# Block-causal attention and a feed-forward pair: the values product of 48 heads taken from whole fp32 operands, two heads side by side

## The chip, the core and the metric

The program runs on one core of one Trainium2 chip. The metric is the device time of one execution in microseconds (us), the median of three runs. One further execution was recorded by the hardware profiler; every row of the trace below is from that one. The engines are TensorE (PE, its weight loads PEld), VectorE (DVE), ScalarE (ACT), GpSimd (POOL) and SyncE (SP), which here only issues DMAs.

## The reference

Eight batches of eight heads, 576 positions, head size 64. Position i sees position j when i's block of 64 is not before j's. The result goes through two dense layers with a leaky ReLU between them:

```
scores = scale * q @ k.T                    # (8, 8, 576, 576), scale = 1/8
scores = where(block_i >= block_j, scores, -1e9)
attn   = exp(scores - max); attn /= sum + 1e-9
x      = attn @ v  -> (4608 tokens, 512)
out    = leaky(x @ w_in) @ w_out            # 512 -> 2048 -> 512, slope 0.01
```

All inputs are fp32.

## The kernel before

**Split operands.** TensorE takes fp32 data in two ways here. An fp32 matmul shows as two matmul records. An "fp32r" matmul shows as one record but keeps fewer bits, so an operand is first split into a high part (a copy into fp32r) and a low part (value minus high part), and a product is built of the partial products. The dense layers work with split operands throughout (`wih`, `wil`, `xh`, `xl`, `gh`, `gl`).

**Heads.** The first 16 heads (`PLAIN`) use whole fp32 operands in the score product (L492) and in the values product (L675); the latter takes two heads at once: head z multiplies with 64 stationary columns and writes PSUM partitions 64z to 64z+63 (`paired`). The other 48, called split heads here, form the scores from split q and k (L503). Their softmax is by DVE (maximum, L524), ACT (exponential, L533) and one of POOL, ACT or DVE (normalising, L562 to L564). The probabilities are turned in 32 x 32 blocks by DVE (L706, tile `turn`), go through DRAM in four DMAs out (L723, `way<-turn`) and four back (L730, `ptm<-way`), and lie in `ptm` with the key on the partitions. Then `ptm` (L738, L739) and the values `v_stage` (L483, L484) are split: four casts and four subtractions per head for `ptm` into `pt`, one of each for `v_stage` into `vs`. These operations have the lines of their helpers in the profile: L263 is a copy or cast on ACT, L264 one on DVE, L273 a subtraction on DVE, L274 one on POOL. The values product of one head is ten fp32r matmuls (L637, L639) with 128 stationary columns (64 of the high part of v, 64 of the low part), so PSUM holds two halves that have to be added: one reduction (L280), two copies (L263 or L264) and four additions (L623, L657) per head bring them into `xr`. There is one `turn`, one `ptm`, one `pt`, one `vs` and one `v_stage`, used by every split head in turn.

**Dense layers.** Tokens go through in 18 chunks of 256. A chunk can start when the batch that holds its last token has been through all eight heads. L793 is the first layer, 3456 matmuls of 256 columns; L820 the second, 1728 of 512.

**The order.** The program is written out by `Plan`, a list scheduler that runs when the kernel is built: each operation has a rank (lower goes first), alternatives by engine, and a modelled duration. Constants set ranks and margins: `RP` for the preparation of q and k, `RT` for the turning, `RM` for its DMAs, `RV` and `RX` for the values product and what follows it, `LEAD` and `LAG` for the dense layers, `PADD` for the margin that it adds after a DMA before it treats an operation as safe to place. Every engine works off its own list strictly in the written order: whatever waits at the head holds up all behind it. SP's list of DMAs is such a list too.

Of the kernel before, what the change touches and what calls it, by code (L numbers as in the profile page):

```python
# [36 lines left out]
RL = -2.043  # L37
RP = 13.059
RB = -31.003
RT = 3.126  # L40
RV = 0.737
RX = 1.288
RN = -97.836
RM = -7.716
RC = 5.009

LEAD = 5.093
LAG = 1.993
RS = -19.813
RG = 1.33  # L50
OFF1 = 3.023
SL1 = 26.175
AHEAD = 2.181
# [5 lines left out]
PADD = 1454.095  # L59
HOLD = 92.996  # L60
FILL = 235
FILLTO = -161.364
# [3 lines left out]
PAD = 426.427  # L66
PADO = 56.068
SPARE = 36.345
CHANGE = 100
RATE = 0.449  # L70
SLOW = 8000


class Plan:
# [37 lines left out]
    def run(self):  # L112
# [14 lines left out]
        start, stream, halved = 0, 0, False  # L127
# [40 lines left out]
        while done < total:  # L168
# [6 lines left out]
            for e, q in ready.items():  # L175
# [29 lines left out]
                name, cost, fn = choices[k]  # L205
# [41 lines left out]
def attention_ffn(ctx: ExitStack, tc: tile.TileContext, q2: bass.AP, k2: bass.AP, qk: bass.AP, v: bass.AP, w_in: bass.AP, w_out: bass.AP, out: bass.AP):  # L247
# [114 lines left out]
    def second_stage():  # L362
        coded.close()
        pool = ctx.enter_context(tc.tile_pool(name="late", bufs=1, side="right", reuse_waits="tile"))
        later["qs"] = fixed([P, S], F32R, "qs", 2, pool)
        later["ks"] = fixed([P, 2, S], F32R, "ks", None, pool)
        later["vs"] = fixed([P, NT, 2 * D], F32R, "vs", None, pool)
        later["v_stage"] = fixed([P, NT, D], F32, "v_stage", None, pool)

    def third_stage():  # L370
        early.close()
        pool = ctx.enter_context(tc.tile_pool(name="last", bufs=1, reuse_waits="tile"))
        later["pt"] = fixed([P, 2, turned], F32R, "pt", None, pool)
        later["ptm"] = fixed([P, turned], F32, "ptm", None, pool)
        later["turn"] = fixed([P, turned], F32, "turn", None, pool)
        xh.append(fixed([P, ND, CH], F32R, "xh1", None, pool))

    def weight_piece(num, rank, f, out_side, c0):
# [28 lines left out]
        if src.dtype != F32:  # L407
# [4 lines left out]
            add([("SP", 475, load)], rank - AHEAD, [], [r_key, t_key], lag="raw")  # L412
# [17 lines left out]
        else:  # L430
# [4 lines left out]
            add([("SP", 475, load)], rank - AHEAD, [], [v_key], lag="raw")  # L435
# [3 lines left out]
    def attention(i):  # L439
# [17 lines left out]
        if plain:  # L457
            kt = lambda: k_in[:, d % 2]
            if z == 0:
                add([("SP", 475, lambda: nc.sync.dma_start(kt(), k2[d]))], early_load, [], [("k", d % 2)], lag="k")  # L460
                add(copying(S, kt, kt, by=scale), rp, [], [("k", d % 2)])
            half = slice(64 * z, 64 * z + 64)
            add([("SP", 475, lambda: nc.sync.dma_start(qk_in[half, z], q2[d, half]))], early_load + 0.05, [], [("q", z)], lag="q")
            vt, vkey = lambda: vf[z], ("vf", z)
            qkd = [("k", d % 2), ("q", z)]
        else:
            add([("SP", 475, lambda: nc.sync.dma_start(qk_in, qk[i - PLAIN]))], r0 - RL, [], ["qkt"], lag="qk")
            vt, vkey = lambda: later["v_stage"], "vt"
        add([("SP", 475, lambda: nc.sync.dma_start(vt(), v[b, h]))], r0 - RL + 0.1, [], [vkey], lag="v")
        if flip:  # L470
# [7 lines left out]
                ))], rp, ["qkt"], [("qs", z)],  # L478
# [30 lines left out]
        def softmax(tiles, mms, masks, r, both=None):  # L509
# [9 lines left out]
            if masks:  # L519
                add([("DVE", sum(82 if len(ap.shape) == 2 else 140 for ap in masks), mask)], r, [], banks)  # L520
# [78 lines left out]
        if plain:  # L599
            if z:  # L600
                paired(b, h // 2, bases, rv, rx)
            return
        ptd = [k for a in range(4) for k in (("pth", bases[a]), ("ptl", bases[a]))]
        vkey = "vs"

        def place(t0, t1):
            r, d = 64 * (h % 2), h // 2

            def ap():
                return xr[b % 2][r : r + 64, d, t0:t1]  # L610

            return ap

        def keys_of(t0, t1):
            return [("x", b % 2, h, y) for y in (0, 1) if (t0 < 320 if y == 0 else t1 > 320)]

        def put_x(x, c, t0, t1, folded=False):
            n, dst, keys = t1 - t0, place(t0, t1), keys_of(t0, t1)
            if folded:
                to = lambda: place(t0, t1)().rearrange("p (e i) -> p e i", i=32)[:, ::-1]  # L620
                of = lambda r: p_t[x][r : r + 64, c : c + n].rearrange("p (e i) -> p e i", i=32)
                add(copying(n, to, lambda: of(64), sb=False), rx, [("t", x)], keys)
                add([("DVE", dve(n), lambda: nc.vector.tensor_add(to(), of(0), to()))], rx, [("t", x)], keys)  # L623
                return
            add(copying(n, dst, lambda: p_t[x][64:128, c : c + n], sb=False), rx, [("t", x)], keys)
            add(
                [("DVE", dve(n), lambda: nc.vector.tensor_add(dst(), p_t[x][0:64, c : c + n], dst()))],
                rx, [("t", x)], keys,
            )

        x0, x1 = bank(b)[0], bank(b)[0]

        def product(dst, j, cols, half, start, stop):

            def go():
                if half == BOTH:
                    nc.tensor.matmul(dst.rearrange("p (y c) -> p y c", y=2), later["vs"][:, j, :], later["pt"][:, :, cols], start=start, stop=stop)  # L637
                    return
                nc.tensor.matmul(dst[:, : cols.stop - cols.start], later["vs"][:, j, :], later["pt"][:, half, cols], start=start, stop=stop)  # L639

            return (2 if half == BOTH else 1) * RATE * (cols.stop - cols.start), go

        b0, b1 = p_t[x0], p_t[x1]
        part = [[
            product(b1, j, slice(c0, c0 + n), y, j == 1 and y == 0, j == 3 and y == 1) for y in range(2)
        ] for j, c0, n in ((1, 0, 512), (2, 512, 448), (3, 1024, 320), (4, 1408, 192))]
        side = product(b0[:, :256], 0, slice(1664, 1792), BOTH, True, True)
        one, two, three, four = part
        add([("PE", [one[0], side, one[1]])], rv, ptd + [vkey], [("t", x0), ("t", x1)])
        add([merging(b0[:, 256:384], b0[:, :256], P)], rx, [], [("t", x0)])  # L650
        add([("PE", [two[0], four[0], two[1], four[1]] + three)], rv, ptd + [vkey], [("t", x1)])
        put_x(x0, 320, 0, 64, True)
        put_x(x1, 0, 64, 576, True)
        late = lambda: place(512, 576)().rearrange("p (e i) -> p e i", i=32)[:, ::-1]
        for r in (0, 64):
            add(
                [("DVE", dve(64), lambda r=r: nc.vector.tensor_add(  # L657
                    late(), p_t[x0][r : r + 64, 256:320].rearrange("p (e i) -> p e i", i=32), late()
                ))],
                rx, [("t", x0)], keys_of(512, 576),  # L660
            )

    def paired(b, d, bases, rv, rx):
# [15 lines left out]
        def put(key, bank, c, a, e, more=False):  # L679
            keys = [("x", b % 2, 2 * d + z, y) for z in range(2) for y in (0, 1) if (a < 320 if y == 0 else e > 320)]  # L680
# [233 lines left out]
```

## Time and profile before

| | |
|---|---|
| runs | 1095.07 us median (1089.72 to 1095.48) |
| profiled execution | 1095.16 us, of which the span of the core is 1093.4 us |
| PE busy | 1057.3 us, 97% |
| DVE busy | 739.2 us, 68% |
| ACT busy | 677.6 us, 62% |
| POOL busy | 455.8 us, 42% |
| mean granted TensorE clock | 0.993 of full speed |
| DMA `ptm<-way`, issue to landing | 4.6 us median (192 issues) |
| DMA `way<-turn`, issue to landing | 2.4 us median (192 issues) |

A matmul's end is modelled in the profile, and matmuls are pipelined, so its recorded duration is longer than the distance to the next one; what a stream of matmuls costs is read from the distance of their starts. PE's idle time is what its busy time leaves of a stretch.

### The profile page before, as it was taken

What the parts mean: (1) busy time and instruction counts of PE and PEld (TensorE: products, weight loads), DVE (VectorE), ACT (ScalarE), POOL (GpSimd) and SP (SyncE); (2) the same over time, 40 slices, a digit from 0 to 9 for tenths busy, and PEclk for the clock granted to TensorE, in tenths of its full rate; (3) what the DMA queues carried; (4) which work ended last, traced back from release to release, by engine and by line L of the source; (5) the groups of instructions that cost most, each with busy time, mean ns of one, the idle gap of its engine ahead of it and who ended that gap; (6) DMA issues with size and microseconds to landing.
All of it is one profiled execution on the core that took longest, in us unless ns stands there. A gap on an engine that the chain in (4) does not pass through costs nothing.

```text
span 1093.4 us, 19734 instructions
## 1 busy us (share of the span) xinstructions
PE 1057.3 (97%) x6736; PEld 940.7 (86%) x6736; DVE 739.2 (68%) x1902; ACT 677.6 (62%) x1621; POOL 455.8 (42%) x414
## 2 busy tenths in 40 slices
PE   6999999999999999999999999999999999999998
PEld 4668888998899889999888989899988999999997
DVE  7999853788799899987556678778987874000000
ACT  6998863776787787867555566577665743222222
POOL 3454321365455535544434354445455431122221
PEclk9999999999999999999999999999998999999999
DMA  5565511676767677676543467447675462000000
GB/s 180 175 191 173 157 52 36 198 204 197 210 191 217 181 209 228 192 217 176 147 127 106 140 188 200 150 138 213 191 201 160 155 181 60 1 20 20 1 20 20
DMA packets 89893, 159.10 MB, mean 146 GB/s; under 512 B 9409, under 2 KB 74945, under 8 KB 89793
## 3 DMA queue, kind: packets, MB, share of 16 engines
q1 hardware_dynamic: 89792, 157.85, 49.4%
q8 instruction: 53, 0.87, 0.4%
q14 instruction: 48, 0.39, 0.1%
HBM read 104.33 MB, written 53.48 MB: 144 GB/s over the span
## 4 chain that ended last, share of the span: by engine, by line
PE 60%; DVE 16%; DMA 10%; ACT 6%; issue 4%; SPq 2%; POOL 0%; DVEq 0%; ACTq 0%; POOLq 0%
PE p_h L793 24%; PE p_o L820 24%; DVE turn L706 4%; DMA ptm<-way 4%; DMA way<-turn 4%; PE p_s L503 4%; DVE nmrec L524 4%; PE p_t L639 3%; ACT prow L533 3%; PE p_s L492 2%; SPq L723 2%; DVE pt L273 1%; PE p_t L589 1%; PE p_t L675 1%; DVE qs L476 1%
## 5 line engine op out<-in xcount | busy, mean ns | idle before, releaser
L793 PE MATMUL p_h<-xh,wih 128*128 128x256 f32 x1152 | 318.1, 281 | 0.6 <-ACT xh L263 0.6
L793 PE MATMUL p_h<-xh,wil 128*128 128x256 f32 x1152 | 316.0, 279 | 0.0
L793 PE MATMUL p_h<-xl,wih 128*128 128x256 f32 x1152 | 301.3, 280 | 0.7 <-DVE xl L273 0.7
L274 POOL TENSOR_TENSOR gl<-g,gh 128x512 fp32r<-128x512 f32 x101 | 133.7, 1324 | 274.1 <-ACT gh L263 206.5
L793 PEld LDWEIGHTS p_h<-xh,wih 128*128 128x128 f32 x1152 | 218.1, 189 | 10.2 <-ACT xh L263 0.8
L793 PEld LDWEIGHTS p_h<-xh,wil 128*128 128x128 f32 x1152 | 218.5, 190 | 0.6
L793 PEld LDWEIGHTS p_h<-xl,wih 128*128 128x128 f32 x1152 | 209.6, 190 | 9.4 <-DVE xl L273 1.0
L533 ACT ACTIVATE prow<-p_s,nmrec 128x448 f32<-128x448 f32 (+1 forms) x300 | 154.3, 524 | 66.7 <-DVE nmrec L524 64.0
L808 ACT ACTIVATE g<-p_h 128x512 f32<-128x512 f32 x144 | 85.5, 594 | 160.5 <-PE p_h L793 160.3
L820 PE MATMUL p_o<-woh,gh 128*128 128x512 f32 x576 | 181.3, 396 | 0.1
L820 PE MATMUL p_o<-wol,gh 128*128 128x512 f32 x576 | 180.4, 394 | 0.0
L820 PE MATMUL p_o<-woh,gl 128*128 128x512 f32 x576 | 179.7, 393 | 0.0
L274 POOL TENSOR_TENSOR pt<-ptm,pt 128x448 fp32r<-128x448 f32 x110 | 135.2, 1250 | 82.8 <-ACT pt L263 37.9
L706 DVE STREAM_TRANSPOSE turn<-prow 128x384 f32<-128x384 f32 (+3 forms) x384 | 146.4, 404 | 28.4 <-DMA way<-turn 9.5
L564 ACT ACTIVATE prow<-prow,nmrec 128x448 f32<-128x448 f32 (+4 forms) x227 | 113.2, 536 | 44.9 <-DVE nmrec L549 42.0
L524 DVE TENSOR_REDUCE nmrec<-p_s 128x1 f32<-128x448 f32 x300 | 129.4, 474 | 2.0 <-issue 0.2
L820 PEld LDWEIGHTS p_o<-woh,gl 128*128 128x128 f32 x576 | 108.7, 189 | 24.7
L820 PEld LDWEIGHTS p_o<-wol,gh 128*128 128x128 f32 x576 | 108.7, 189 | 23.8
L503 PE MATMUL p_s<-ks,qs 128*128 128x288 f32 (+4 forms) x528 | 93.5, 311 | 15.3 <-ACT prow L533 15.2
L263 ACT CAST pt<-ptm 128x448 fp32r<-128x448 f32 x158 | 82.0, 565 | 37.1 <-DMA ptm<-way 31.9
L562 POOL TENSOR_SCALAR prow<-prow,nmrec 128x576 f32<-128x576 f32 (+4 forms) x76 | 52.9, 697 | 111.1 <-DVE nmrec L549 80.4
L503 PEld LDWEIGHTS p_s<-ks,qs 128*128 128x128 f32 x528 | 78.9, 191 | 23.2 <-ACT prow L533 19.5
(90 smaller groups left out, 1433.8 us busy)
## 6 DMA issues: line engine op xcount, KB each, us to landing
way<-turn SPq DMA_DIRECT2D x192, 224.0 KB, 2.4
ptm<-way SPq DMA_DIRECT2D x192, 224.0 KB, 4.6
qk_in<-in_qk SPq DMA_DIRECT2D x48, 576.0 KB, 4.6
out<-ob SPq DMA_DIRECT2D x35, 256.0 KB, 3.0
raw<-in_w_in SPq DMA_DIRECT2D x16, 512.0 KB, 4.3
raw<-in_w_out SPq DMA_DIRECT2D x16, 512.0 KB, 4.1
v_stage<-in_v SPq DMA_DIRECT2D x48, 160.0 KB, 3.7
vf<-in_v SPq DMA_DIRECT2D x16, 160.0 KB, 4.1
```

Source lines behind the costliest of these rows:

```text
L263: one = lambda: nc.scalar.copy(dst(), src())
L274: ("POOL", pool2(n), lambda: nc.gpsimd.tensor_sub(dst(), one(), two())),
L503: nc.tensor.matmul(ap, later["qs"][z][:, cols], moving, start=first, stop=last)
L524: [("DVE", dve(kw[t]), lambda t=t, ap=ap, flat=flat: nc.vector.tensor_reduce(nm[z][: qn[t], at_col[t] : at_col[t] + 1], ap[: qn[t]], axis= ...
L533: nc.scalar.activation(o, ap[: qn[t]], AF.Exp, bias=nm[z][: qn[t], at_col[t] : at_col[t] + 1], scale=1.0, accum_out=sums[z][: qn[t], at_co ...
L562: ("POOL", pool1(kw[t]), lambda: nc.gpsimd.tensor_scalar(p(), p(), by, 1.0, op0=ALU.mult, op1=ALU.mult)),
L564: ("ACT", act(kw[t], True) + 108, lambda: nc.scalar.mul(p(), p(), by)),
L639: nc.tensor.matmul(dst[:, : cols.stop - cols.start], later["vs"][:, j, :], later["pt"][:, half, cols], start=start, stop=stop)
L706: nc.vector.transpose(dst, src.rearrange("p (s b i) -> p s b i", b=4, i=32))
L793: nc.tensor.matmul(p_h[z][:, i, :], w[:, d, f * P : (f + 1) * P], (xl if x else xh[y])[:, d, :], start=first and k == 0 and (u > 0 or i == ...
L808: add([("ACT", act(512), lambda: nc.scalar.activation(g, p_h[z], AF.Prelu, alpha=0.01))], rank, [("h", z)], ["g"])
L820: nc.tensor.matmul(p_o[m], a[:, i, m * P : (m + 1) * P], w[:, 2 * u + i, :], start=u == 0 and k == 0, stop=u == NU - 1 and k == 5,)
```

## The change

For the 48 split heads the values product now takes `ptm` and the values as they land, in whole fp32, and two heads at once in the two column halves of TensorE, as `paired` does it for the first 16. The operations that split `ptm` and `v_stage`, and those that add the two halves of PSUM, are gone with the tiles `pt` and `vs`. `turn` and `ptm` become two tiles each, one for each head of a pair; `v_stage` becomes `vt`, also two. The seven products of a head (instead of ten matmuls) read `ptm` in blocks of 32, two to four runs at a time; some write PSUM in runs with gaps. One transpose (`flipped` of tile 4, block 13) takes 128 partitions instead of 64. The scheduler's constants are all new, it adds 110 ns in its model where DVE changes between two kinds of operation (`EDGE`), and reckons 530 instead of 475 ns for a DMA's issue (`ISSUE`). The number of DMAs stays.

```diff
-RP = 13.059
-RB = -31.003
-RT = 3.126
-RV = 0.737
-RX = 1.288
-RN = -97.836
-RM = -7.716
-RC = 5.009
-LEAD = 5.093
+RP = 20.774
+RB = -3.305
+RT = 2.986
+RV = -1.976
+RX = -2.769
+RN = -66.464
+RM = -40.088
+LEAD = 4.317
...
-PADD = 1454.095
+PADD = 3219.925
...
+EDGE = 110
+ISSUE = 530
...
-        later["vs"] = fixed([P, NT, 2 * D], F32R, "vs", None, pool)
-        later["v_stage"] = fixed([P, NT, D], F32, "v_stage", None, pool)
...
-        later["pt"] = fixed([P, 2, turned], F32R, "pt", None, pool)
-        later["ptm"] = fixed([P, turned], F32, "ptm", None, pool)
-        later["turn"] = fixed([P, turned], F32, "turn", None, pool)
+        later["ptm"] = fixed([P, turned], F32, "ptm", 2, pool)
+        later["turn"] = fixed([P, turned], F32, "turn", 2, pool)
+        later["vt"] = fixed([P, NT, D], F32, "vt", 2, pool)
...
-            vhd, vld = (lambda y=y: later["vs"][:, :, y * D : (y + 1) * D] for y in range(2))
-            add(copying(NT * D, vhd, vt, fast=False), rp, [vkey], ["vs"])
-            add(subtracting(NT * D, vld, vt, vhd, "POOL"), rp, [vkey], ["vs"])
...
+        if z:
+            (paired(b, h // 2, bases, rv, rx) if plain else columns(b, h // 2, rv, rx))
+
+    def put(b, d, rx, key, bank, c, a, e, more=False, back=False):
+        keys = [("x", b % 2, 2 * d + z, y) for z in range(2) for y in (0, 1) if (a < 320 if y == 0 else e > 320)]
+        to, of = (lambda: xr[b % 2][:, d, a:e]), (lambda: bank[:, c : c + e - a])
+        if back:
+            to = lambda: xr[b % 2][:, d, a:e].rearrange("p (t a i) -> p a t i", a=4, i=32)[:, :, ::-1]
+            of = lambda: bank[:, c : c + e - a].rearrange("p (a t i) -> p a t i", a=4, i=32)
+        if more:
+            add([("DVE", dve(e - a), lambda: nc.vector.tensor_add(to(), of(), to()))], rx, [key], keys)
+        else:
+            add(copying(e - a, to, of, sb=False), rx, [key], keys)
+
+    def columns(b, d, rv, rx):
+        ptd = [("ptm", z, g) for z in range(2) for g in range(4)] + [("vt", z) for z in range(2)]
+        _, k0, t0 = bank(b)
+        _, k1, t1 = bank(b)
+
+        def product(to, j, s0, s1, a0, a1, start, stop):
+            n, w = (a1 - a0) * (s1 - s0) * 32, (s1 - s0) * 32
+
+            def go(z):
+                src = later["ptm"][z].rearrange("p (a s) -> p a s", a=4)[:, a0:a1, 32 * s0 : 32 * s1]
+                dst = to[64 * z : 64 * z + 64].rearrange("p (a s) -> p a s", a=4)[:, a0:a1, :w]
+                nc.tensor.matmul(dst, later["vt"][z][:, j], src, start=start, stop=stop)
+
+            return [(2 * RATE * n, lambda z=z: go(z)) for z in range(2)]
+
+        values = [
+            product(t1, 1, 0, 4, 0, 4, True, False),
+            product(t0[:, :P], 0, 13, 14, 0, 4, True, True),
+            product(t1, 2, 4, 8, 2, 4, False, False),
+            product(t1, 3, 8, 10, 0, 2, False, False),
+            product(t1, 4, 11, 13, 0, 4, False, False),
+            product(t1, 2, 4, 7, 0, 2, False, False),
+            product(t1, 3, 8, 11, 2, 4, False, True),
+        ]
+        add([("PE", [y for x in values for y in x])], rv, ptd, [k0, k1], kind="half")
+        put(b, d, rx, k0, t0, 0, 0, 64)
+        put(b, d, rx, k1, t1, 0, 64, 576, back=True)
+        put(b, d, rx, k0, t0, 64, 512, 576, True)
...
-        for a in range(4):
-            part = lambda y, a=a: later["pt"][:, y].rearrange("p (s a i) -> p a s i", a=4, i=32)[:, 3 - a]
-            hi, lo = lambda part=part: part(0), lambda part=part: part(1)
-            raw = lambda a=a: later["ptm"][:, a * w : (a + 1) * w].rearrange("p (s i) -> p s i", i=32)
-            add(copying(w, hi, raw), r0 + RC, got, [("pth", bases[a])])
-            add(subtracting(w, lo, raw, hi), r0 + RC, got + [("pth", bases[a])], [("ptl", bases[a])])
```

## Rows read from the trace of the kernel before

**Rows 1.** Busy time by stretch: engines' busy us (instructions), granted clock, DMA share, GB/s
```profile
0.00:100.00 100.00, 84.59 (x497) 61.54 (x498) 88.59 (x234) 86.92 (x225) 41.48 (x57) 1.00 0.59 181
...
200.00:900.00 700.00, 683.21 (x4367) 621.95 (x4366) 569.67 (x1479) 478.01 (x1162) 342.27 (x300) 0.99 0.63 182
```
**Rows 2.** Busy time by stretch, the three stretches with a lowered clock
```profile
500.00:600.00 100.00, 96.30 (x616) 87.53 (x616) 63.07 (x160) 56.71 (x132) 43.74 (x36) 0.98 0.52 144
600.00:700.00 100.00, 95.90 (x604) 86.54 (x603) 76.11 (x191) 62.24 (x155) 45.69 (x42) 0.98 0.59 168
800.00:900.00 100.00, 97.12 (x612) 88.70 (x611) 81.41 (x211) 61.41 (x148) 47.15 (x41) 0.97 0.59 171
```
**Rows 3.** Waits of PE: who for whom, us in total, times, longest
```profile
PE p_s L503 <- ACT prow L533: 15.2, 12, 2.9
```
**Rows 4.** Timeline of PE around its longest wait: start, us, instructions [idle before]
```profile
822.57 1.97 PE L503 MATMUL p_s<-ks,qs 128*128 128x288 f32 x7 [2.88 <-ACT prow L533]
...
826.90 1.05 PE L820 MATMUL p_o<-woh,gh 128*128 128x512 f32 x2
```
**Rows 5.** Timeline of DVE ahead of that wait
```profile
817.26 0.68 DVE L623 TENSOR_TENSOR xr<-p_t,xr 64x512 f32<-64x512 f32 x1
...
820.22 1.02 DVE L524 TENSOR_REDUCE nmrec<-p_s 128x1 f32<-128x448 f32 x2
```
**Rows 6.** Waits of SP's DMA queue and of DVE: us in total, times, longest
```profile
SPq L469 <- POOL vs L274: 36.9, 24, 5.5
...
DVE turn L706 <- DMA way<-turn: 9.5, 10, 2.3
```
**Rows 7.** The chain that ended last, pieces of it: start, us, what
```profile
545.92 5.33 DMA ptm<-way
...
551.35 0.57 ACT pt L263
...
567.16 4.45 DMA out<-ob
...
674.70 6.82 DMA ptm<-way
```
**Rows 8.** Timeline of PE: a values product of two plain heads, one of a split head
```profile
117.70 2.91 PE L675 MATMUL p_t<-ptf,vf 128*64 128x512 f32 x20
...
118.61 0.39 PE L675 MATMUL p_t<-ptf,vf 128*64 128x128 f32 x4
...
118.83 0.55 PE L675 MATMUL p_t<-ptf,vf 128*64 128x448 f32 x2
...
120.55 0.73 PE L820 MATMUL p_o<-woh,gh 128*128 128x512 f32 x2
121.12 0.63 PE L820 MATMUL p_o<-wol,gh 128*128 128x512 f32 x2
...
309.56 0.39 PE L639 MATMUL p_t<-pt,vs 128*128 128x512 f32 x1
...
311.07 0.62 PE L820 MATMUL p_o<-woh,gh 128*128 128x512 f32 x2
311.52 0.62 PE L820 MATMUL p_o<-wol,gh 128*128 128x512 f32 x2
```
**Rows 9.** Groups of instructions by line: busy us, mean ns | idle before, releaser
```profile
L274 POOL TENSOR_TENSOR pt<-ptm,pt 128x448 fp32r<-128x448 f32 x110 | 135.2, 1250 | 82.8 <-ACT pt L263 37.9 <-DVE pt L264 34.0 <-DVE nmrec L548 6.0
...
L263 ACT CAST pt<-ptm 128x448 fp32r<-128x448 f32 x158 | 82.0, 565 | 37.1 <-DMA ptm<-way 31.9 <-issue 3.4 <-POOL gl L274 1.5
...
L273 DVE TENSOR_TENSOR pt<-ptm,pt 128x448 fp32r<-128x448 f32 x82 | 66.3, 834 | 4.1 <-ACT pt L263 3.4
...
L623 DVE TENSOR_TENSOR xr<-p_t,xr 64x64 f32<-64x64 f32 x96 | 42.9, 447 | 6.6 <-ACT xr L263 4.2
...
L274 POOL TENSOR_TENSOR vs<-v_stage,vs 128x320 fp32r<-128x320 f32 x39 | 35.6, 913 | 56.9 <-ACT vs L263 33.1 <-issue 17.7 <-DVE vs L264 3.7
...
L280 DVE TENSOR_REDUCE p_t<-p_t 128x128 f32<-128x256 f32 x48 | 19.5, 406 | 9.2 <-PE p_t L637 9.1
```

More of the change, by code (lines that the diff above doesn't have):

```diff
@@ L126, in run @@
         order, now, moved, done = [], 0, 0, 0
-        start, stream, halved = 0, 0, False
+        start, stream, halved, edge = 0, 0, False, 0
         def offer(i):
@@ L204, in run @@
                 choices, _, _, lag, _ = self.ops[i]
-                name, cost, fn = choices[k]
+                name, cost, fn = choices[k][:3]
+                if e == "DVE":
+                    near, far = choices[k][3] if len(choices[k]) > 3 else (0, 0)
+                    cost += EDGE * (near != edge)
+                    edge = far
                 free[e] = now + cost + SPARE
@@ L519, in softmax @@
             if masks:
-                add([("DVE", sum(82 if len(ap.shape) == 2 else 140 for ap in masks), mask)], r, [], banks)
+                add([("DVE", sum(82 if len(ap.shape) == 2 else 140 for ap in masks), mask, (2, 0))], r, [], banks)
             for t, ap, bk in tiles:
@@ L598, in attention @@
         rv, rx = r0 + RV, r0 + RX
[L599 to L661, printed above, removed]
+        if z:
+            (paired(b, h // 2, bases, rv, rx) if plain else columns(b, h // 2, rv, rx))
@@ L706, in go @@
                 nc.vector.transpose(dst, src.rearrange("p (s b i) -> p s b i", b=4, i=32))
-            add([("DVE", dve(k * P), go)], r0 + RT, pkeys(t), [("turn", t, j)])
-        flipped(0, 13, 14, 1, 0, 0, 64)
+            add([("DVE", dve(k * P), go)], r0 + RT, pkeys(t), [("turn", z, t, j)] + ([("turn", z, 4, 4)] if t == 0 else []))
         flipped(1, 3, 8, 4, 0, k=2)
@@ L855, in attention_ffn @@
         if i == PLAIN:
-            new = [("qs", y) for y in range(2)] + ["kh", "kl", "vs", "vt"]
+            new = [("qs", y) for y in range(2)] + ["kh", "kl"]
             add([("POOL", 1, second_stage)], 0, [y for k in wkeys.values() for y in k], new)
-            new = [("turn", t, j) for t, j in ((0, 0), (1, 0), (2, 0), (3, 0), (3, 3), (4, 0), (4, 3), (4, 4))]
-            new += [(y, g[0]) for g in tgroups for y in ("pth", "ptl")] + [("ptm", b) for b in range(4)] + ["qkt"]
+            blocks = ((0, 0), (1, 0), (2, 0), (3, 0), (3, 3), (4, 0), (4, 3), (4, 4))
+            new = [("turn", y, t, j) for y in range(2) for t, j in blocks]
+            new += [("ptm", y, b) for y in range(2) for b in range(4)] + [("vt", y) for y in range(2)] + ["qkt"]
             new += [("xh", 1, e) for e in range(0, CH, BLK)]
```

71 lines of the change are left out of this document (31 added, 40 removed).

## Prediction

> **What bounds the kernel now.** I read the busy time by stretch first. TensorE is busy nearly always: in the 700 us from 200 to 900, in which the split heads and the dense layers run side by side, it lacks only 700 - 683.2 = 16.8 us [rows 1], and no other engine comes near (DVE 569.7 us). The reader is to see that the bound is the stream of matmuls: work saved on DVE, ACT or POOL is worth at most what TensorE now waits or loses, and work added to TensorE is paid in full.
>
> Second, TensorE's waits. Twelve waits of score matmuls for ACT's exponential, 15.2 us in total, the longest 2.9 us, are nearly the whole of that idle time [rows 3]: the next scores need the PSUM banks that the exponential of the scores before has not yet read. Third, what a wait costs besides itself. After the longest one a pair of L820 matmuls takes 1.05 us [rows 4] where it takes 0.62 in an undisturbed place [rows 8]: the granted clock had fallen to its lower level. Three stretches show a mean clock of 0.98, 0.98 and 0.97 [rows 2]. Full speed is 2.4 GHz and the lower level half of it, so a mean of 0.98 is 4 us of 100 at half speed, of which half is lost: 2 + 2 + 3 = 7 us. What can be won between 200 and 900 is 16.8 + 7 = 23.8 us.
>
> Fourth, the chain of waits: why the exponentials are late. Each engine works in written order, so the maximum and the exponential stand behind whatever waits ahead of them. One wait of the twelve: `ptm` lands 5.3 us after its issue, ACT has the cast of `ptm` at the head of its list and idles for it, and only then come the exponentials for which TensorE waits [rows 7]. The longest: the maximum at 820.2 stands behind the 0.7 us addition of PSUM halves and others like it [rows 5]. Of the ten longest gaps of TensorE I followed back in the chain, eight pass through an operation that the change takes away (a split of `ptm` or v, an addition of halves, a transpose that waits for the only `turn`); two start at the landing of a result row (`out<-ob`, 4.5 us [rows 7]) for which a copy of the next one waits, and these stay.
>
> **The change part by part.** The sum is made against the profiled execution: span 1093.4 us, 1.8 us outside it, 1095.2 in all. The median of the runs is 1095.1, so the two need no correction.
>
> *The values product.* Before, a split head's runs from 309.56 to 311.07, 1.51 us, two heads 3.02 us [rows 8]. The price of the new form is that of the plain pair, which is the same kind of matmul: it starts at 117.70, the next matmul at 120.55, and that one's pair takes 0.57 instead of 0.45 us to the next start, so 0.12 us more belongs to the switch: 2.97 us for 1600 columns a head [rows 8]. By piece: 512 columns 0.91 us, 128 columns 0.22 us (118.61 to 118.83). The new pair has 512 + 128 + 256 + 128 + 256 + 192 + 192 = 1664 columns a head: 0.91 + two times 0.22 + two times 0.43 + two times 0.33 + 0.2 for the switch at the end = 3.07 us. That is 0.05 us more per pair, 24 pairs: +1.2 us. Low end: every column at the best rate seen, 0.22 / 128 = 1.7 ns, no switch, gives 2.83 us, 24 x -0.19 = -4.6 us. High end: each of the seven products pays the 0.12 us of the switch, 2.97 x 1664 / 1600 + 6 x 0.12 = 3.81 us, 24 x 0.79 = +19 us. I take +1.2, since the plain pair already has one short product between long ones, at no extra cost.
>
> The 128-column product in rows 8 reads its moving operand in two runs of 64 and still streams at 0.22 us, so gaps in what is read cost nothing there; gaps in what is written no row shows. The Trainium skill, PSUM — Partial Sum Buffer, Specifications (TRN2), says that PSUM's lines are of 8 bytes and that a non-contiguous pattern slows matmuls significantly. By that rule the products that write runs of 64 or 96 columns would be slowed, which the sum above does not have; the rival further down gives it a time.
>
> *The splits and the additions of halves.* Six groups go whole: 135.2 + 82.0 + 66.3 us for `ptm`, 35.6 for v on POOL, 42.9 and 19.5 for the halves: 381.5 us [rows 9], beside smaller ones. That is over a quarter of the 569.7 + 478.0 + 342.3 = 1390 us that the three engines are busy from 200 to 900 [rows 1]. None of it is on TensorE's list, so it is worth nothing by itself; it is worth the waits it causes. What comes instead per pair is two copies and one addition, as for plain heads, about 1.2 us by the 0.68 us of 512 columns [rows 5] and two short ones, 24 x 1.2 = 29 us, in the room made free.
>
> *Two `turn` tiles and two values tiles.* DVE waits 9.5 us in ten places for `way<-turn` before it may write `turn` again [rows 6]; with a second tile the landing has a whole head's time. SP's load of v waits 36.9 us for POOL's split of v [rows 6], and the DMAs behind it on SP's list, `way<-turn` among them, wait with it. Now the load waits for the values product of the pair before. DVE would be late next for q and k, and for the output copies.
>
> *The new wait.* The values matmuls now wait on TensorE's own list for the landing of both heads' `ptm`. Queued behind are all scores and dense matmuls. Where the order leaves 5 us between issue and product it costs nothing: the cover is the dense work between. If the cover is gone, a late landing (6.8 us instead of 5.3 [rows 7]) costs 1.5 us and the clock that follows. Low end 0; high end is in the rivals. I take 0, because the landing to be covered is one that ACT and DVE now wait for with less time behind it: a cast of 0.6 and a subtraction of 1.3 us [rows 9], 1.8 us together, fall away from the path.
>
> *The order.* The constants change every place in the lists, also in the first 100 us, where TensorE lacks 15.4 us [rows 1] and DVE and ACT are nearly full. None of the removed work lies there. Nothing in the trace prices the new order: I take 0, with 5 us, a third of that idle time, either way.
>
> *Sum.* Of the 23.8 us, the share of gaps that pass through a removed operation is eight in ten; but a gap closed in one place lets the next late operation show, so I count two thirds: -16. With +1.2 for TensorE: 1095.2 - 16 + 1.2 = 1080.4 us. Its own range, from a third of the waits gone (-8) with +5 on TensorE to all of them gone with -4.6: 1067 to 1092.
>
> **The rivals.**
>
> *Nothing waits any more.* With a quarter or more of their work gone, DVE and ACT are never late, and the new order also gains up to 5 us at the start. For it: DVE's 569.7 us of 700, 81% [rows 1], fall to 63% by the 66.3, 42.9 and 19.5 us of rows 9 alone. Against: the `out<-ob` gaps have nothing to do with the change. 1095.2 - 23.8 + 1.2 = 1072.6, with the start 1067.6.
>
> *The waits only move.* The order is made from modelled durations and DMAs land when they land. For it: the busiest stretches are not those with the longest waits (500 to 600 has DVE at 63% and TensorE at 96.3 [rows 2]), so load is not the only cause. Against: the chain at these places does run through `ptm`. Then 1095.2 + 1.2 = 1096.4, give or take 3.
>
> *Slower: TensorE itself waits for `ptm`.* Place: the head of each values product. Price: 1.5 us late plus as much again in lower clock (after the 2.9 us wait the clock is still low 4.3 us after TensorE goes on, at a pair of 1.05 us: 5.4 us at half speed lose 2.7 [rows 4]), 3 us each; it decides from the point where more than five of the 24 pairs are late, since five cost the 16 us saved. Half of the pairs late: 12 x 3 = 36, 1095.2 + 1.2 - 16 + 36 = 1116. For it: one landing of 6.8 us, and SP issues these DMAs one after another behind others. Against: twelve waits before, none of them on TensorE's list for a DMA.
>
> *Slower: PSUM with gaps.* 768 of the 1664 columns are written in runs with gaps. If these take twice their time, 768 x 1.7 ns = 1.3 us a pair, 24 x 1.3 = 31 us: 1080.4 + 31 = 1111. Against: the runs are 64 and 96 columns long, and the nearest row, reading in runs of 64, shows full rate. This is the skill's PSUM rule carried through; no run here has shown it.
>
> **How the numbers follow.** A measurement of this kernel can tell some 0.5% from no change, 5.5 us: faster is below 1089.6, slower above 1100.5. The forecast gets 0.46, "nothing waits" 0.24, "only move" 0.19, the two slower ones 0.07 and 0.04. Nearly all of the forecast's share and all of the second are faster: 0.70. The third is within, with a little of the first: 0.18. Slower: the last two and a bad order, 0.12. The range leaves out what is beyond 1098 above (the slower ones), and below it goes to the second rival with 7 us more from the start: 1060 to 1098.
>
> **What would show it.** In the profile of the changed kernel: the values pair at about 3.07 us from first start to the next matmul's; waits of score matmuls for the exponential down to 5 us or less between 200 and 900; a granted clock of 0.99 or more in all stretches there; busy time of POOL and DVE in that stretch down by 130 and 100 us at least. The prediction is wrong if TensorE's pair takes 3.5 us or more, if it waits for `ptm` at the values product, or if the score waits stay at 15 us with the three engines a quarter lighter.

## The result and the profile after

| | before | changed |
|---|---|---|
| median of the runs | 1094.17 us (4 runs) | 1078.87 us (4 runs, 1077.18 to 1080.17) |
| ratio, 95% interval | | 0.9866 (0.9833 to 0.9899) |
| profiled execution, its span | 1095.16, 1093.4 us | 1080.17, 1078.4 us |
| mean granted clock | 0.993 | 0.995 |
| DVE, ACT, POOL busy | 739.2, 677.6, 455.8 us | 598.7, 554.3, 237.1 us |

The forecast was 1080.4, so the time came out as predicted. Its terms did not all do so: two errors in opposite directions nearly cancelled, and the experiments leave the reason behind the largest term only partly shown.

Busy time by stretch of the changed kernel (TensorE, its weight loads, DVE, ACT, POOL, granted clock, DMA share, GB/s), as in [rows 1, 2]:

```profile
0.00:100.00 100.00, 82.48 (x464) 60.45 (x466) 80.32 (x213) 84.03 (x221) 37.44 (x55) 0.95 0.54 162
...
200.00:900.00 700.00, 696.25 (x4735) 610.91 (x4733) 443.97 (x1271) 366.34 (x903) 135.30 (x106) 1.00 0.65 186
...
500.00:600.00 100.00, 100.00 (x675) 87.85 (x674) 46.93 (x132) 48.52 (x111) 19.16 (x14) 1.00 0.49 144
600.00:700.00 100.00, 99.76 (x672) 87.31 (x673) 63.79 (x182) 53.51 (x132) 18.31 (x15) 1.00 0.66 190
...
800.00:900.00 100.00, 98.82 (x672) 87.18 (x670) 59.00 (x167) 47.12 (x115) 15.64 (x12) 1.00 0.63 179
...
60.00:80.00 20.00, 16.85 (x102) 11.91 (x99) 17.64 (x43) 18.45 (x46) 8.40 (x7) 0.91 0.65 189
```

Two things are to be seen. From 200 to 900 TensorE now lacks 3.75 us instead of 16.8, and the three stretches that had a lowered clock have 1.00: the gain is 13.0 + 7 = 20 us.

In the first 100 us it went the other way: 17.5 us idle instead of 15.4, and more time at the lower clock. How much more can't be read from the clock column there (0.95 against 1.00). For the first matmuls it shows 1.00 in both kernels, but their recorded times are 1.7 to 1.9 times those of the same matmuls at full speed. The changed kernel:

```profile
4.38 2.90 PE L492 MATMUL p_s<-k_in,qk_in 128*128 128x448 f32 x4 [4.38 <-DMA qk_in<-in_q]
7.08 1.55 PE L492 MATMUL p_w<-k_in,qk_in 128*128 128x448 f32 x4
12.87 3.25 PE L492 MATMUL p_s<-k_in,qk_in 128*128 128x288 f32 x8 [4.25 <-ACT prow L533]
15.91 2.47 PE L492 MATMUL p_w<-k_in,qk_in 128*128 128x288 f32 x8
```

The kernel before:

```profile
4.64 2.93 PE L492 MATMUL p_s<-k_in,qk_in 128*128 128x448 f32 x4 [4.64 <-ACT k_in L266]
7.36 2.57 PE L492 MATMUL p_w<-k_in,qk_in 128*128 128x448 f32 x4
11.72 1.73 PE L492 MATMUL p_s<-k_in,qk_in 128*128 128x288 f32 x8 [1.79 <-ACT prow L533]
```

The fast rows are 1.55 us for four matmuls of 448 columns and 1.73 for eight of 288. Against these the changed kernel loses 1.35 + 1.52 + 0.74 = 3.6 us in the rows shown, the kernel before 1.38 + 1.02 = 2.4: 1.2 us more. From 60 to 80 a mean clock of 0.91 is 3.6 us at half speed, 1.8 us lost, where the kernel before has 1.00. With the 2.1 us of idle time the first 100 us cost 2.1 + 1.2 + 1.8 = 5.1 us more.

TensorE's waits for the exponential from 200 to 900 us in the changed kernel (us in total, times, longest), as in [rows 3]:

```profile
PE p_s L503 <- ACT prow L533: 3.7, 5, 1.2
```

The waits of the split heads' scores (L503) are 3.7 us in five places where they were 15.2 in twelve. TensorE's other waits of any size (L492, 7.5 + 4.9 + 4.4 us) are for the plain heads in the first 100 us. No row has a values matmul that waits for `ptm`; one of its weight loads waited 0.4 us for a DMA.

The values pair on TensorE (start, us, instructions), as in [rows 8]:

```profile
311.17 0.63 PE L782 MATMUL p_o<-wol,gh 128*128 128x512 f32 x2
311.64 0.62 PE L782 MATMUL p_o<-woh,gl 128*128 128x512 f32 x2
312.19 3.03 PE L624 MATMUL p_t<-ptm,vt 128*64 128x512 f32 x28
...
313.10 0.39 PE L624 MATMUL p_t<-ptm,vt 128*64 128x128 f32 x4
...
313.32 0.60 PE L624 MATMUL p_t<-ptm,vt 128*64 128x256 f32 x4
...
313.75 0.39 PE L624 MATMUL p_t<-ptm,vt 128*64 128x128 f32 x4
...
313.97 0.60 PE L624 MATMUL p_t<-ptm,vt 128*64 128x256 f32 x4
...
315.15 1.13 PE L503 MATMUL p_s<-ks,qs 128*128 128x288 f32 x7
```

The same seven score matmuls in the kernel before, behind a dense matmul:

```profile
307.33 1.03 PE L503 MATMUL p_s<-ks,qs 128*128 128x288 f32 x7
```

From 312.19 to 315.15 are 2.96 us, and so it is for all 24 pairs of the trace. The switch between the two forms of matmul costs something beside that, on both sides. On the way in, the dense pair at 311.64 takes 0.55 us to the next start where the one before it takes 0.47: 0.08 us. On the way out, the score matmuls recorded 1.13 us instead of 1.03: 0.1 us. Together 3.14 us a pair, where the kernel before has 3.02 for two heads [rows 8]. Those are nine matmuls a head in the trace (L637 once, L639 eight times), not ten as the section on the kernel before says; the time read from the starts is the same.

The first 128-column product (313.10 to 313.32) writes PSUM without gaps, the second (313.75 to 313.97) in runs of 64 columns: both 0.22 us.

### The profile page after: what moved, and what is told of

The parts are those of the page before. It is cut to its first block, busy times and chain, and to the rows that moved or that the text cites. A ratio compares the mean times of both kernels' runs of the same rounds, so it can differ in the third digit from the quotient of the medians.

```text
span 1078.4 us, 19058 instructions
## 1 busy us (share of the span) xinstructions
PE 1053.0 (98%) x6976; PEld 912.6 (85%) x6976; DVE 598.7 (56%) x1649; ACT 554.3 (51%) x1335; POOL 237.1 (22%) x209
## 4 chain that ended last, share of the span: by engine, by line
PE 86%; DMA 5%; ACT 4%; DVE 3%; issue 1%; SPq 0%; ACTq 0%; DVEq 0%
PE p_h L755 34%; PE p_o L782 33%; PE p_s L503 6%; PE p_t L624 6%; DMA qk_in<-in_qk 3%; PE p_s L492 3%; ACT prow L533 2%; PE p_t L589 1%; PE p_t L654 1%; DVE turn L677 1%; DMA raw<-in_w_out 1%; DVE nmrec L524 1%; DMA raw<-in_w_in 1%; DMA out<-ob 1%; ACT prow L564 0%
## 5 line engine op out<-in xcount | busy, mean ns | idle before, releaser
L279 POOL TENSOR_TENSOR gl<-g,gh 128x512 fp32r<-128x512 f32 x115 | 149.5, 1300 | 674.0 <-ACT gh L268 509.5
L533 ACT ACTIVATE prow<-p_s,nmrec 128x448 f32<-128x448 f32 x300 | 154.3, 524 | 91.6 <-DVE nmrec L524 84.6
L677 DVE STREAM_TRANSPOSE turn<-prow 128x384 f32<-128x384 f32 (+3 forms) x384 | 141.9, 399 | 11.7 <-ACT prow L564 7.8
L564 ACT ACTIVATE prow<-prow,nmrec 128x320 f32<-128x320 f32 (+4 forms) x152 | 78.6, 531 | 36.2 <-DVE nmrec L549 36.2
L503 PE MATMUL p_s<-ks,qs 128*128 128x288 f32 (+4 forms) x528 | 92.7, 309 | 3.7 <-ACT prow L533 3.7
L782 PEld LDWEIGHTS p_o<-woh,gh 128*128 128x128 f32 x576 | 89.8, 188 | 3.5 <-issue 1.3
L503 PEld LDWEIGHTS p_s<-ks,qs 128*128 128x128 f32 x528 | 77.9, 189 | 13.5 <-ACT prow L533 5.7
L278 DVE TENSOR_TENSOR xl<-xr,xh 128x1024 fp32r<-128x1024 f32 (+3 forms) x24 | 23.1, 968 | 110.0 <-PE p_h L755 110.0
L268 ACT CAST gh<-g 128x512 fp32r<-128x512 f32 x107 | 66.3, 620 | 18.2 <-PE p_o L782 16.5
```

The costliest lines, as they stand in the source:

```text
L268: one = lambda: nc.scalar.copy(dst(), src())
L279: ("POOL", pool2(n), lambda: nc.gpsimd.tensor_sub(dst(), one(), two())),
L503: nc.tensor.matmul(ap, later["qs"][z][:, cols], moving, start=first, stop=last)
L533: nc.scalar.activation(o, ap[: qn[t]], AF.Exp, bias=nm[z][: qn[t], at_col[t] : at_col[t] + 1], scale=1.0, accum_out=sums[z][: qn[t], at_co ...
L564: ("ACT", act(kw[t], True) + 108, lambda: nc.scalar.mul(p(), p(), by)),
L677: nc.vector.transpose(dst, src.rearrange("p (s b i) -> p s b i", b=4, i=32))
```

## The experiments

All are timed in three rounds or more beside the kernel before on the same chip; the ratio is to that. The chips differ between experiments, so kernels are compared by the ratio. "Score waits" are those of L503 (or the same line under another number) for the exponential between 200 and 900 us.

| kernel | median us | ratio, 95% interval | TensorE busy from 200 to 900, us | score waits, us |
|---|---|---|---|---|
| before | | 1 | 683.2 | 15.2 |
| changed | 1078.87 | 0.9866 (0.9833 to 0.9899) | 696.3 | 3.7 |
| form_old_order | 1080.37 | 0.9867 (0.9845 to 0.9889) | 692.9 | 3.8 |
| old_form_new_order | 1088.87 | 0.9937 (0.9915 to 0.9960) | 689.4 | 6.9 |
| before_nudge | 1089.90 | 0.9943 (0.9918 to 0.9968) | 684.2 | 13.8 |
| old_form_margin | 1093.83 | 0.9978 (0.9953 to 1.0003) | 688.6 | 10.0 |
| one_turn | 1084.14 | 0.9902 (0.9881 to 0.9923) | 691.6 | 2.7 |
| load_back | 1074.13 | 0.9815 (0.9791 to 0.9839) | 699.7 | 0.3 |
| load_planned | 1072.79 | 0.9814 (0.9797 to 0.9832) | 699.2 | 0.8 |
| load_fixed | 1083.10 | 0.9902 (0.9876 to 0.9928) | 693.8 | 5.9 |
| probe_fixed | 1082.23 | 0.9895 (0.9870 to 0.9921) | 696.5 | 3.3 |
| load_probe_fixed | 1113.51 | 1.0153 (1.0093 to 1.0212) | 671.4 | 27.5 |
| raw_first | 1078.29 | 0.9866 (0.9847 to 0.9885) | 696.9 | 2.7 |
| halves_apart | 1126.60 | 1.0283 (1.0232 to 1.0334) | 699.8 | 0.2 |

### Form or order

**form_old_order**: the changed kernel with the old constants.

```diff
-RL = -1.611
+RL = -2.043
...
-PADD = 3219.925
+PADD = 1454.095
...
-EDGE = 110
-ISSUE = 530
+EDGE = 0
+ISSUE = 475
```

> The new values product with all constants of the order as before the change. If the gain is that the splits and the additions of halves are gone from the lists (theory), the waits of score matmuls for the exponential between 200 and 900 us stay at 6 us or less and the time is 1076 to 1086. If the gain is the new order (rival), the waits are 12 us or more and the time is 1090 or more.

The stretch and TensorE's longest waits in it:

```profile
200.00:900.00 700.00, 692.92 (x4708) 606.80 (x4707) 387.43 (x1116) 371.00 (x925) 213.94 (x206) 1.00 0.65 185
...
PE p_s L503 <- ACT prow L533: 3.8, 6, 1.3
PE p_o L782 <- ACT ob L268: 3.3, 2, 2.5
```

As the theory had it: the score waits are gone with the old constants too, and the whole gain is there (0.9867). What is left beside them is TensorE's wait for the copy of a result row.

**old_form_new_order**: the kernel before with all the new constants and `EDGE` and `ISSUE`.

```diff
-PADD = 1454.095
+PADD = 3219.925
...
-LEAD = 5.093
+LEAD = 4.317
...
+                    cost += EDGE * (near != edge)
...
```

> The old values product, splits and one turn tile, with the constants and the two model terms (EDGE, ISSUE) of the change. Theory (operations gone): 1088 to 1102, score waits between 200 and 900 us of 10 us or more. Rival (the order, above all the larger margin after a DMA): 1085 or less, score waits of 6 us or less.

```profile
200.00:900.00 700.00, 689.36 (x4455) 628.66 (x4454) 599.64 (x1535) 475.15 (x1158) 342.87 (x296) 1.00 0.64 184
...
PE p_s L509 <- ACT prow L539: 6.9, 7, 2.0
```

Between the two: time inside the theory's range, waits under it. The order alone takes 0.6% of the time. About half of the score waits are gone in the profiled execution, but at 1084.5 us that is the fastest of six. Form and order don't add (1.3% and 0.6% alone, 1.3% together).

**before_nudge** asks how much of such a step is chance: the kernel before with one number of the scheduler's model, added to the time of each operation, a nanosecond larger. After that every engine's list comes out different in detail; the work, the ranks and the margins after DMAs stay.

```diff
-SPARE = 36.345
+SPARE = 37.345
```

> The kernel before with one constant of the scheduler's model, SPARE, raised by 1 ns (36.345 to 37.345), so that an order comes out that is as good as the old one by every rank and margin, but different in detail on every engine. If the waits belong to the old form: 1090 to 1100, within 0.5% of the kernel before. If the order's detail is worth as much as the form: off by 0.5% or more either way, and score waits between 200 and 900 us off by 5 us or more.

The stretch, and the score waits in it:

```profile
200.00:900.00 700.00, 684.19 (x4398) 622.16 (x4398) 575.56 (x1499) 468.16 (x1140) 346.57 (x309) 1.00 0.64 183
...
PE p_s L503 <- ACT prow L533: 13.8, 13, 2.0
```

It is 0.6% faster, as the second expectation had it, with nearly the score waits of before, as the first had it, and TensorE 1 us busier; its clock is 1.00 in the stretch where before has 0.99. So a step of half a per cent by a new order means little here. The four kernels of the old form lie at 0.994 to 1, the four of the new form that differ in order alone (changed, form_old_order, raw_first, load_planned) at 0.981 to 0.987: the form is worth more than that scatter, the order not shown to be.

**old_form_margin**: the kernel before with the new margin after a DMA.

```diff
-PADD = 1454.095
+PADD = 3219.925
```

> The kernel before with one constant changed: PADD, the margin that the scheduler adds after a DMA before it treats an operation as safe to place, 1454 to 3220 ns. If the larger margin is what the new order gained with the old form (0.6%): 1085 to 1091, ACT and DVE waiting 25 us or less for ptm instead of 48. If it is the other constants, or chance: 1092 to 1100.

The waits of ACT and DVE for `ptm` in it:

```profile
ACT pt L263 <- DMA ptm<-way: 29.0, 21, 4.4
DVE pt L264 <- DMA ptm<-way: 7.7, 7, 2.4
```

And in the kernel before:

```profile
ACT pt L263 <- DMA ptm<-way: 31.9, 22, 4.2
DVE pt L264 <- DMA ptm<-way: 16.6, 13, 3.2
```

36.7 us instead of the 48.5 of before, 1093.8 us: no gain outside the interval, and not the 25 us or less expected of the margin. The larger margin alone is not what the new order gained.

### Load or waiting place

The forecast gave two reasons for the late exponentials at once: the engines' load, and that a split stands at the head of a list and waits for `ptm`. Five runs take them apart.

**load_back**: the casts and subtractions planned and executed again, on zeros, for nobody.

```diff
...
+        for a in range(4):
+            hi, raw = (lambda: later["ds"]), (lambda: later["ds"].bitcast(F32))
+            add(copying(w, hi, raw), r0 + RC, got, ["ds"])
+            add(subtracting(w, hi, raw, hi), r0 + RC, got, ["ds"])
...
```

> The changed kernel with the four casts and four subtractions of 448 columns per split head put back as work on a tile of zeros that nobody reads, placed after the landing of ptm: the load of the splits without their place on the path to the values product. If load makes the waits: 1086 to 1096, score waits of 8 us or more. If it is the place on the path: 1077 to 1083, score waits of 5 us or less, with POOL and DVE some 130 and 70 us busier.

```profile
200.00:900.00 700.00, 699.73 (x4768) 615.00 (x4768) 512.93 (x1364) 443.08 (x1068) 251.83 (x234) 1.00 0.65 186
...
PE p_s L506 <- ACT prow L536: 0.3, 1, 0.3
```

DVE is 69 us, ACT 77 and POOL 117 us busier than in the changed kernel, and TensorE waits for nearly nothing: 1074 us, faster than either expectation. The added work does not wait for `ptm`, as the splits did. Load alone therefore does not bring the waits. But the scheduler had written another order.

**load_planned** keeps that order and leaves the work out.

```diff
...
+        none = lambda: None
+        for a in range(4):
+            add(copying(w, none, none), r0 + RC, got, ["ds"])
+            add(subtracting(w, none, none, none), r0 + RC, got, ["ds"])
+            plan.ghosts.update(range(len(plan.ops) - 2, len(plan.ops)))
...
-                order.append(fn)
+                if i not in self.ghosts:
+                    order.append(fn)
```

> The changed kernel written out in the order of load_back, that is with the splits in the scheduler's plan but left out of the program. If load_back was fast because of the order that came out of its plan: 1070 to 1077, and TensorE busy over 698 of the 700 us from 200 to 900. If the extra work itself helped (it cannot by the theory of load): 1077 to 1083, as the changed kernel.

```profile
200.00:900.00 700.00, 699.15 (x4760) 614.32 (x4761) 441.72 (x1251) 373.88 (x918) 132.41 (x111) 1.00 0.65 186
```

1072.8 us: the order made load_back fast, and the work that came with it cost nothing measurable. With load_back this is the fastest kernel of the study, 0.5% under the changed one.

The next three keep the changed kernel's own order on every list and only insert. **load_fixed** inserts work that waits for nothing:

```diff
...
+        out = [(2000 * k, lambda: nc.scalar.copy(a(), a())) for k in range(6)]
+        out += [(1700 * k + 300, lambda: nc.vector.tensor_sub(d(), d(), d())) for k in range(7)]
+        return out + [(2000 * k + 600, lambda: nc.gpsimd.tensor_sub(p(), p(), p())) for k in range(6)]
```

> The changed kernel in its own order, not planned anew, with work added on tiles that nothing else reads: per split head 6 operations of 160 columns on ACT, 7 on DVE, 6 on POOL, spread over 12 us after the modelled landing of ptm; about the load of the removed splits, waiting for nothing. If load makes the waits: 1084 to 1096, score waits between 200 and 900 us of 8 us or more. If it is the waiting place on the lists: 1077 to 1083, score waits of 6 us or less.

```profile
200.00:900.00 700.00, 693.77 (x4704) 606.23 (x4703) 568.54 (x1599) 424.13 (x1183) 282.88 (x387) 1.00 0.65 186
...
PE p_s L510 <- ACT prow L540: 5.9, 8, 1.7
```

DVE is as busy as before the change (568.5 us, [rows 1]: 569.7), ACT at 424 of 478, POOL at 283 of 342. The time rises by 0.36 points of the ratio, 4 us, between the two expectations; the intervals of this kernel and of the changed one overlap, so the rise is not clear of the noise.

**probe_fixed** inserts nearly no work, but the wait:

```diff
...
+            (0, lambda: nc.scalar.copy(later["da"], later["ptm"][z][:, 0:32])),
+            (0, lambda: nc.vector.tensor_copy(later["dd"], later["ptm"][z][:, 0:32])),
```

> The changed kernel in its own order with one tiny copy of 32 columns of ptm on ACT and one on DVE per split head, placed at the modelled landing of ptm: next to no load (48 x 0.2 us on each), but ACT and DVE wait again for the DMA at the head of their lists, as the splits made them. If the waiting place is what the change took away: 1083 to 1096, ACT and DVE waiting 15 us or more each for ptm, score waits between 200 and 900 us of 8 us or more. If load is: 1077 to 1082, score waits of 5 us or less.

The waits of ACT and DVE for `ptm` in it, and TensorE's for the exponential from 200 to 900:

```profile
DVE dd L857 <- DMA ptm<-way: 51.6, 35, 6.6
ACT da L856 <- DMA ptm<-way: 47.2, 32, 3.4
...
PE p_s L509 <- ACT prow L539: 3.3, 7, 0.8
```

ACT and DVE wait for `ptm` as long as before the change and longer, and the scores don't wait more than in the changed kernel. The time rises by 0.29 points, 3 us, again within overlapping intervals; in the profiled execution, 1078.66 us, the fastest of the four, nothing of it is to be seen. Neither reason alone carries the gain of 15 us.

**load_probe_fixed** inserts both.

```diff
...
+            (0, lambda: nc.scalar.copy(a()[:, 0:32], later["ptm"][z][:, 0:32])),
+            (0, lambda: nc.vector.tensor_copy(d()[:, 0:32], later["ptm"][z][:, 0:32])),
...
+        out += [(2000 * k, lambda: nc.scalar.copy(a(), a())) for k in range(6)]
+        out += [(1700 * k + 300, lambda: nc.vector.tensor_sub(d(), d(), d())) for k in range(7)]
+        return out + [(2000 * k + 600, lambda: nc.gpsimd.tensor_sub(p(), p(), p())) for k in range(6)]
```

> The changed kernel in its own order with both additions at once: the load of load_fixed and the two small copies of ptm at its modelled landing of probe_fixed. If load and waiting place act through each other (an engine that is late because it waited has no room to catch up): 1086 to 1094, score waits between 200 and 900 us of 9 us or more. If they only add, or the rest of the gain is the order: 1081 to 1086, score waits of 5 to 8 us.

```profile
200.00:900.00 700.00, 671.42 (x4481) 581.50 (x4480) 546.00 (x1568) 414.01 (x1176) 272.62 (x370) 0.99 0.62 177
...
PE p_s L510 <- ACT prow L540: 27.5, 26, 3.7
...
DVE dd L859 <- DMA ptm<-way: 53.4, 26, 5.1
ACT da L858 <- DMA ptm<-way: 48.9, 25, 4.7
```

4 us and 3 us alone, neither clear of the noise; together 2.9 points of the ratio, 31 us, and that is clear: beyond the range expected, in its direction. The waits for `ptm` are as long as in probe_fixed, but now 26 waits of scores follow, and the clock falls again. The likely reason is that an engine with this load cannot make up what it lost before the next exponential is due; no run shows that step by itself. The loss is twice what the change gained. Here the order was not made for this work, whereas in the kernel before the scheduler had placed the exponentials with the splits in view; that this makes the difference is not shown either.

So the two together can bring the waits back in this order. Whether they are what made the waits of the kernel before is another question, and its trace says: only in part. Within the 8 us ahead of its twelve score waits, ACT or DVE wait for `ptm` ahead of two, 2.1 of the 15.2 us. In before_nudge it is seven of thirteen, 8.6 of 13.8 us; in old_form_margin two of nine, 3.4 of 10.0 us; in load_probe_fixed 14 of 26, 15.1 of 27.5 us. Ahead of other long waits of the kernel before an engine waits for another DMA:

```profile
297.23 0.58 DVE L706 STREAM_TRANSPOSE turn<-prow 128x384 f32<-128x384 f32 x1 [2.33 <-DMA way<-turn]
...
571.73 0.69 DVE L264 COPY ob<-p_o 128x512 f32<-128x512 f32 x1 [4.47 <-DMA out<-ob]
...
814.19 0.69 ACT L266 ACTIVATE qs<-qk_in 128x576 fp32r<-128x576 f32 x1 [2.16 <-DMA qk_in<-in_qk]
```

The score waits that follow are 1.7 us at 301.0, 2.0 at 575.0 and 2.9 at 822.6, 6.6 of the 15.2 us. The landings of result rows and of q and k have nothing to do with the change. No run puts back the additions of halves, the split of v with the wait that it causes on SP's list, or the single `ptm`, and none has the splits wait for `ptm` in an order planned for them with the rest of the new form. What each of these had in the waits stays open.

### The smaller parts

**one_turn**: one `turn` tile.

```diff
-        later["turn"] = fixed([P, turned], F32, "turn", 2, pool)
+        later["turn"] = fixed([P, turned], F32, "turn", None, pool)
...
```

> The changed kernel with one turn tile instead of two. Theory (the second tile is a small part): 1079 to 1084, and DVE waits 5 to 12 us in total for way<-turn again. Rival (the second tile is what takes the waits away): 1088 or more, score waits of 10 us or more between 200 and 900 us.

```profile
DVE turn L677 <- DMA way<-turn: 27.1, 19, 3.8
```

DVE waits 27.1 us for the tile, more than twice what was expected, against 0.7 us with two. Score waits stay low (2.7 us); TensorE's busy time falls to 691.6 us. The time is 0.36 points up, at the upper edge of the theory's range; since the order is planned anew, that is within what a nudge does, and the share of the second tile in the gain stays open.

**raw_first**: the first load of weights ahead of the loads of v.

```diff
-            add([("SP", ISSUE, load)], rank - AHEAD, [], [r_key, t_key], lag="raw")
+            add([("SP", ISSUE, load)], rank - AHEAD - (2 if num == 0 else 0), [], [r_key, t_key], lag="raw")
...
```

> The changed kernel with the first load of weights two ranks earlier, ahead of the loads of v on SP's list. In the changed kernel TensorE waits 4.3 us at 12.9 us for an exponential that stands on ACT's list behind the coding of these weights. Theory: that wait falls under 2.5 us and the time by 1 to 5 us, to 1074 to 1078. Rival: the place is taken by another wait in the first 100 us, or the order planned anew loses it elsewhere: 1078 to 1084.

TensorE's waits at the start:

```profile
11.88 3.23 PE L492 MATMUL p_s<-k_in,qk_in 128*128 128x288 f32 x8 [2.46 <-ACT prow L533]
...
18.68 1.82 PE L492 MATMUL p_s<-k_in,qk_in 128*128 128x448 f32 x2 [1.87 <-ACT prow L533]
```

The wait of 4.3 us is 2.5 us now, and the next one grew to 1.9: the rival. The time is that of the changed kernel. Not even the shorter wait is clearly the work of the edit: halves_apart, load_fixed, probe_fixed and load_probe_fixed begin with the lists of the changed kernel, and there the same wait took 3.0, 3.6, 3.1 and 2.7 us.

**halves_apart**: the two heads of a pair one after the other.

```diff
-        add([("PE", [y for x in values for y in x])], rv, ptd, [k0, k1], kind="half")
+        add([("PE", [x[z] for z in range(2) for x in values])], rv, ptd, [k0, k1], kind="half")
```

> The changed kernel with the values products of a pair in another order on TensorE: all seven of the first head, then all seven of the second, instead of the two heads by turns. All else stays in place. If two column halves run side by side only where their matmuls follow each other (theory): a pair takes 5.7 to 6.1 us instead of 3.0, 24 x 2.8 = 67 us more, 1135 to 1155 with the waits that this shifts. If TensorE overlaps the halves over a longer stretch of its queue: 1078 to 1090.

```profile
316.11 5.24 PE L624 MATMUL p_t<-ptm,vt 128*64 128x512 f32 x28
321.27 0.98 PE L503 MATMUL p_s<-ks,qs 128*128 128x288 f32 x6
```

5.16 us instead of 2.96, 24 x 2.2 = 53 us; measured 48 us over the changed kernel by the medians, 46 by the ratio. The score waits are down to 0.2 us, likely because TensorE has longer between scores, which would account for some of the difference. So the theory holds in the main, and its numbers were too high: a pair is cheaper than the 5.7 us expected, and the time lies 8 us below the range given.

## Why the prediction was right, point by point

**TensorE is the bound and its waits are what can be won.** Right. 23.8 us were seen to be there; 20 were won in that stretch, and in load_planned TensorE lacks 0.9 us of 700. The four signs that the prediction named for this all came: the pair, score waits of 3.7 us, a clock of 1.00, and POOL and DVE 207 and 126 us less busy.

**The values pair, +1.2 us in all.** The forecast's 3.07 us a pair was close, but it left out the switch on the way in: 3.14 us against 3.02 before is 24 x 0.12 = +2.9 us. halves_apart shows that this price needs the two heads by turns.

**The rival of gaps in PSUM.** Not so here: 0.22 us with runs of 64 as without, and 0.43 us for 256 columns either way (313.32 to 313.75 without gaps, 313.97 to 314.40, where the next product starts, in runs of 64). 192 columns in runs of 96 take 0.33 us (314.40 to 314.72), the same 1.7 ns a column. The Trainium skill's statement in PSUM — Partial Sum Buffer, Specifications (TRN2), that a non-contiguous pattern slows matmuls significantly, is not what these rows show, and the measurement decides for runs this long.

**TensorE waiting for `ptm`.** Did not come: no such row but the 0.4 us of one weight load.

**The waits, -16 us.** The size was 4 us short; 20 lies as near to the rival "nothing waits any more" (23.8) as to the forecast. The step that failed is "a gap closed in one place lets the next late operation show", for which 8 us were set aside: the stretch is nearly without waits, and of the gaps behind result rows, which were to stay, one of 0.5 us is left. That the gain is the form's is shown by form_old_order. The reason is shown only in part. The prediction had the removed work "worth the waits it causes", and gave its load and its place on the lists at once. By load_back and load_planned the load of casts and subtractions costs nothing measurable once it is planned for. By load_fixed and probe_fixed, in a fixed order, the load adds 4 us and the wait for `ptm` 3, neither clear of the noise. By load_probe_fixed both together cost 31. But ahead of ten of the twelve waits of the kernel before neither ACT nor DVE had waited for `ptm` in the last 8 us, so this pair of causes does not account for the whole.

What the changed kernel still waits for fits the remark in the prediction that q, k and the output copies would be late next. ACT's waits for the landing of q and k, before and after:

```profile
ACT qs L266 <- DMA qk_in<-in_qk: 7.0, 9, 2.2
```

```profile
ACT qs L271 <- DMA qk_in<-in_qk: 47.2, 27, 4.5
```

ACT now waits longer for q and k than it did for `ptm` (31.9 us). Four of the five score waits that are left come within 8 us behind such a wait, the fifth behind a result row. But all five are only 3.7 us. So a late landing does show where another was closed, but here it costs TensorE little.

**The order, 0 with 5 us either way.** In the profiled execution the first 100 us cost 5.1 us more, at the edge of those 5. One part of it: the first weights are now loaded behind v, ACT waits longer for them, and their coding stands ahead of the first exponential on ACT's list. The changed kernel, and the kernel before:

```profile
9.76 0.66 ACT L271 ACTIVATE val<-raw 128x512 f32<-128x512 f32 x1 [5.59 <-DMA raw<-in_w_in]
```

```profile
7.39 0.66 ACT L266 ACTIVATE val<-raw 128x512 f32<-128x512 f32 x1 [2.81 <-DMA raw<-in_w_in]
```

Some of the 5.1 us is that execution's own. halves_apart, load_fixed and probe_fixed have the same lists in this stretch, and there TensorE lacks 16.6, 15.7 and 15.9 us instead of 17.5, with a clock of 0.97 or 0.98 instead of 0.95. The mean clock over the span is 0.998 in two of the changed kernel's other three executions against 0.995 in the profiled one. For the rest of the kernel the nudge shows that a new order moves the time by half a per cent without any reason that a row of before could have told.

**The sum.** -13.0 - 7 + 5.1 + 2.9 = -12.0, and the span fell by 15.0 us. So the time came within 2 us of the forecast partly by luck: 4 us more were won between 200 and 900 than forecast, and 5.1 lost at the start, where the forecast had nothing. 3.0 us are left over. A pair of 512-column matmuls is recorded at 0.62 us where the next starts after 0.45 [rows 8], so each wait costs some 0.17 us more than the idle time shown; seven waits fewer are 1.2 us of it. The clock's two decimals hold up to 1.5 us either way. The rest is open.

## What to carry to other kernels

An operation that waits for a DMA at the head of an in-order list can be cheap on an engine with room and dear on a busy one (here 3 us and, with the load, 31, in one fixed order): read the wait and the load together. Before crediting a wait, look what stood ahead of each gap of the bounding engine: a total of 48.5 us of waiting for `ptm` lay ahead of only two of twelve. Where a program's order is made by a scheduler, run a nudged copy before believing half a per cent, and try the order of a neighbouring plan: here the order planned with work that was then left out was the fastest.

## Not expected

- One nanosecond per operation in the scheduler's model changed the time by 0.57% (0.9943, 0.9918 to 0.9968).
- Waiting place and load: +3 and +4 us alone, neither clear of the noise, +31 us together.
- One head after the other, the two column halves still overlap at the seam: the second head's first product starts at 318.32, beside the last two of the first head, and the pair takes 5.16 us, less than twice 2.96.

```profile
318.32 0.65 PE L624 MATMUL p_t<-ptm,vt 128*64 128x512 f32 x3
```
